# Scores of the first four head pairs as one fp32 product, with new orders of the steps: threshold attention followed by a two-layer MLP

## The chip, the cores and the metric

The kernel runs on one core of one Trainium2 chip. Its engines each work through their own queue in order and wait for one another through semaphores: TensorE (PE in the profile; its weight loads are PEld), VectorE (DVE), ScalarE (ACT), GpSimd (POOL) and SyncE (SP), of which SP and POOL here issue nearly all DMAs. The metric is the device time of one execution in microseconds (us). Three runs of the kernel before gave 519.77, 519.93 and 520.16 us, so the median is 519.93 us.

## The reference

Attention with a threshold: of each row of scores only those within tau (0.02) of the row's maximum stay, the others are masked. Then a two-layer MLP with a leaky ReLU. There are 8 batches, 8 heads, 576 positions, 64 values a head, so 64 heads, which are handled as 32 pairs; 4608 tokens of width 512, and a hidden width of 2048.

```python
scores = scale * np.matmul(q, k.transpose(0, 1, 3, 2))          # scale = 1/8
thresh = np.max(scores, axis=-1, keepdims=True) - tau
scores = np.where(scores >= thresh, scores, -1000000000.0)
scores = scores - np.max(scores, axis=-1, keepdims=True)
attn = np.exp(scores)
attn = attn / (np.sum(attn, axis=-1, keepdims=True) + 1e-09)
attn_out = np.matmul(attn, v)
x = attn_out.transpose(0, 2, 1, 3).reshape(B * S, H * D)
h = x @ w_in
out = np.maximum(0.01 * h, h) @ w_out
```

Since a score close to the threshold may fall on either side of it, the scores are needed more exactly than one fp16 product gives them.

## The kernel before, in words

Two heads make a pair (`p`, 0 to 31), and two pairs make a couple (`c`, 0 to 15). A couple has nine blocks `t` of scores: 0 to 3 are 128 query rows each of its first pair, 4 to 7 those of its second, and block 8 holds the last 64 rows of both. One pass of the main loop is a step `(c, t)`; a last pass with `c = 16` finishes what is left.

`load_qk` brings q and k of a pair into the tile `nat`, by SP's queue. `prep(p, i)` turns q (`i = 0`) or k (`i = 1`) on TensorE with an identity matrix, for the first ten pairs as plain fp32 products of 64 columns (line 151), into a pair of PSUM banks (tag `A`, of which there is one; tag `s` for the very first k). A copy on ACT scaled by 64 makes `hi` in fp16 (line 172), and a subtraction on DVE makes the rest `lo`, also in fp16 (line 175). The copy is put on the list `due`, which the letter `h` of the order runs, and the subtraction on the list `soon`, which `L` runs.

`s_mm` (line 196) makes one block of scores for both heads: for each half of the 576 columns hi times hi, lo times hi and hi times lo are added up in PSUM, for two heads side by side in the rows 0 to 63 and 64 to 127 of the array. There are two buffers `s`, one for each head, so a new block waits until DVE has read the one before. Where the step's number is in a list in line 190, the first head's six products go ahead of the second's.

`s_max` (letters `0` and `1` for the two heads) reads a block on DVE into `sn` with its extreme `nmx` (line 221), and POOL makes the threshold `nth` (line 226). Then either ACT takes the exponential `e` (line 231) and DVE masks it one step later in `s_mask` (letter `M`, line 254), or, "direct", ACT does both in `far` and `W` (lines 237 and 241). `s_mask` also issues the transposing DMA of the weights on SP (line 261). After a couple is done, its sums (`d`, `r`, `x`, `T`, `Q0`, `Q1`) and its products with v (`values`, `V0` and `V1`, line 329) follow in the next one.

MLP work comes in units: `h_unit` (four products of 512 columns, line 354, and a copy `gM` on ACT) and `out_mm` (four products, line 369; every fourth is followed by a copy on ACT and a store). The units of a batch are pushed in step 6 of every second couple from couple 2 on. `share` says how many units a step gets, `up` how they are split between the letters `U` and `u`, with `w` for one more. `filler(n)` issues n products of no use (line 126, letter `f` in the loop), with numbers for the couples 0, 1 and 2 alone.

The order of everything is written out by hand: `orders[cl][t]` is a string of these letters for each step, with `cl` = 0, 1, 2 for the first three couples, 3 for later odd ones and 4 for later even ones. Letters that work on different engines only meet through data; letters on the same engine queue up as the string has them. POOL issues the loads of v (line 107) and of the MLP weights (lines 116 and 120), ten of v's right at the start after a small copy `begun` from the first q.

Of the kernel before, what the change touches and what calls it, by code (L numbers as in the profile page):

```python
# [9 lines left out]
FP32 = mybir.dt.float32  # L10
FP16 = mybir.dt.float16
OP = mybir.AluOpType
AF = mybir.ActivationFunctionType
# [3 lines left out]
def kernel(  # L17
# [10 lines left out]
    nc = tc.nc  # L28
    B, H, S, D = q.shape
# [5 lines left out]
    NT = 9  # L35
    NJ = d_ff // 128
    QS = 64.0
# [4 lines left out]
    sb = ctx.enter_context(tc.tile_pool(name="sb", bufs=1))  # L42
# [17 lines left out]
    nat, qk, wTs, xTs = {}, {}, {}, {}  # L60
# [61 lines left out]
    def filler(n):  # L122
        if n > 0:
            t = bank()
            for _ in range(n):
                nc.tensor.matmul(out=t[:, :], lhsT=gM[:, 0, 0:128], rhs=gM[:, 0, :], start=True, stop=True,  # L126
                                 skip_group_check=True)
# [14 lines left out]
    def prep(p, i, tag="A", bufs=1):  # L142


        t = nat[p]
        pt = pair_of_banks(tag, bufs)
        for c in range(4 + i):

            if p < 10:
                for r, h in ((0, 0), (1, 0), (0, 1), (1, 1)):  # L150
                    nc.tensor.matmul(  # L151
                        out=pt[ds(64 * h, 64), r, ds((0, 2, 1, 3, 4)[c] * 64, 64)],
                        lhsT=by_head(t, i)[ds(64 * r, 64), h, c, :] if c < 4 else t[ds(64 * r, 64), 8, h, :],
                        rhs=I32[ds(64 * r, 64), ds(64 * r, 64)],
                        start=True, stop=True, skip_group_check=True,
                    )
                continue
            for r in range(2):
                nc.tensor.matmul(  # L159
                    out=pt[0:128, r, ds((0, 2, 1, 3, 4)[c] * 64, 64)],  # L160
                    lhsT=t[ds(64 * r, 64), 4 * i + c, :, :].rearrange("p h d -> p (h d)"),
                    rhs=I32[ds(64 * r, 64), ds(64 * r, 64)],
                    is_transpose=True, skip_group_check=True,
                )
# [5 lines left out]
        hi = sb.tile([128, N], FP16, tag=f"hi{i}", bufs=3, name=f"hi{i}")  # L170
        lo = sb.tile([128, N], FP16, tag=f"lo{i}", bufs=3, name=f"lo{i}")
        due.append(lambda: (nc.scalar.activation(out=by_half(hi[:, :]), in_=src, func=AF.Copy, bias=0.0, scale=QS), was.add(("hi", p, i)), soon.append(rest)))  # L172
        def rest():
            assert ("hi", p, i) in was
            nc.vector.scalar_tensor_tensor(  # L175
                out=by_half(lo[:, :]), in0=src, scalar=QS, in1=by_half(hi[:, :]),
                op0=OP.mult, op1=OP.subtract,
            )
            was.add(("lo", p, i))
        qk.setdefault(p, {})[i] = (hi, lo)  # L180

    def s_mm(c, t):


        out = [ps.tile([128, 2, 512], FP32, tag="s", bufs=2, name="s") for _ in range(2)]
        if t < 8:
            srcs = [(2 * c + t // 4, 0, ds(t % 4 * 128, 128), ds(0, 128))]
        else:
            srcs = [(2 * c + e, 1, ds(576, 64), ds(64 * e, 64)) for e in range(2)]
        hs = ((0,), (1,)) if c * NT + t in [3, 9, 10, 22, 26] else ((0, 1),)  # L190
        for hh, half in ((x, y) for x in hs for y in range(2)):
            for ti, (a, b) in enumerate(((0, 0), (1, 0), (0, 1))):
                for p, i, cols, po in srcs:
                    for h in hh:
                        r = ds(h * 64, 64)
                        nc.tensor.matmul(  # L196
                            out=out[h][po, half, 0:288], lhsT=qk[p][i][a][r, cols],
                            rhs=qk[p][1][b][r, ds(half * 288, 288)],
                            start=(ti == 0), stop=(ti == 2), skip_group_check=True,
                        )  # L200
# [233 lines left out]
    with tc.manual_schedule():  # L434
# [27 lines left out]
        share = (23, 24, 32, 13, 17, 10, 26, 35, 23, 23, 24, 26, 13, 23, 13, 26, 35, 23)  # L462
        up = [[1, 3, 2, 3, -1, -1, -1, 2, -1], [1, 3, 0, 3, -1, 1, 1, 2, -1], [2, 2, 0, 2, -3, 2, -1, 1, -1], [2, 3, 1, -1, -3, 3, -1, 1, -3], [3, 2, 0, -1, -3, 3, -1, 1, 1]]
# [3 lines left out]
        orders = [['S Pe f h 0 1 M L', 'S f h 0 1 M L', 'Pd h S f 0 1 M L', 'S 0 1 M L f', 'S f 0 L 1 M', 'S Pa f h 0 1 M L', 'S f Pb h 0 1 M L', 'S f 0 h 1 M L', 'S f 0 Pc h 1 M L'], ['S f 0 w Pd h U 1 u M L d r', 'S f 0 h x 1 u U w T L M', 'S f 0 Q0 M h U 1 u L', 'S U f 0 w V0 1 u M L', 'S f 0 U Q1 L h 1 M u', 'S f 0 1 u V1 M U L', 'S Pa f h 0 U 1 u M L', 'S f 0 U Pb w h u 1 M L', 'U S f 0 Pc h w 1 u M L'], ['S Pd f h U 0 h 1 M d L u', 'w r S f 0 U x u T h 1 M L', 'S f w L 0 Q0 h 1 U M u', 'S V0 f 0 1 M u U L w', 'S f Q1 0 U 1 h u L M', 'S f 0 V1 1 u w M U L', 'G S 0 f 1 Pa h U u M L', 'f Pb S 0 U h 1 M w u L', 'S f 0 U Pc h u M 1 L'], ['S Pd h U 0 h 1 M d w u L', 'r S 0 U x T u 1 w h L M', 'S U Q0 h 0 u 1 M L', 'S V0 0 1 u M U L', 'S 0 w L U Q1 h 1 M u', 'S V1 0 U 1 u L M', 'G S U Pa h 0 u w 1 M L', 'S 0 U Pb h u M 1 L', 'S 0 Pc h u U 1 M L w'], ['S Pd h U 0 h 1 M d w u L', 'S r 0 U x u w T h 1 M L', 'S U Q0 h 0 1 M L u', 'S V0 0 u 1 M U L w', 'S 0 w L U Q1 h 1 M u', 'S V1 0 U 1 u L M', 'G S 0 Pa U h u w 1 M L', 'S 0 U Pb h 1 u M L w', 'S 0 Pc h u U 1 M L']]  # L467
        credit = 0.0
        plan = {}

# [16 lines left out]
        for c in range(NC + 1):  # L487
            last = c == NC
            for t in range(NT):
# [21 lines left out]
                for o in orders[cl][t].split():  # L511
# [90 lines left out]
```

## Time and profile before

The profiled execution took 519.91 us, of which the profile's span is 518.1 us.

| what | number |
|---|---|
| median of three runs | 519.93 us |
| profiled execution | 519.91 us (span 518.1) |
| TensorE busy | 496.3 us, 96% |
| VectorE busy | 419.7 us, 81% |
| ScalarE busy | 428.2 us, 83% |
| GpSimd busy | 208.7 us, 40% |
| mean granted clock of TensorE | 0.988 |

In the rows of a timeline the first number is the start in us, the second the length of the group, then engine, line, instruction, and what is written from what; a bracket at the end is the idle time ahead of it on its engine and what ended it. A group row of the page ends with its count, busy time, mean in ns, and the idle time before it. The chain of waits follows the work back from the last instruction, at each step to what released it.

### The profile page before, as it was taken

What the parts mean: (1) busy time and instruction counts of PE and PEld (TensorE: products, weight loads), DVE (VectorE), ACT (ScalarE), POOL (GpSimd) and SP (SyncE); (2) the same over time, 40 slices, a digit from 0 to 9 for tenths busy, and PEclk for the clock granted to TensorE, in tenths of its full rate; (3) what the DMA queues carried; (4) which work ended last, traced back from release to release, by engine and by line L of the source; (5) the groups of instructions that cost most, each with busy time, mean ns of one, the idle gap of its engine ahead of it and who ended that gap; (6) DMA issues with size and microseconds to landing.
All of it is one profiled execution on the core that took longest, in us unless ns stands there. A gap on an engine that the chain in (4) does not pass through costs nothing.

```text
span 518.1 us, 14182 instructions
## 1 busy us (share of the span) xinstructions
PE 496.3 (96%) x5277; PEld 268.0 (52%) x5277; DVE 419.7 (81%) x1094; ACT 428.2 (83%) x777; POOL 208.7 (40%) x471
## 2 busy tenths in 40 slices
PE   7788888999999999999999999999999999999996
PEld 4354544555545565554545465555555465545444
DVE  6797998998899889987999889988999889982000
ACT  3788996988899888999898888999898888983622
POOL 6454467543553236323553336323643336320000
PEclk9798999999999999999999999999999999999999
DMA  8999999997999799988998699996998899644112
GB/s 186 162 184 185 193 174 214 176 178 133 198 179 170 134 182 174 175 149 152 180 176 159 137 185 189 158 168 134 179 174 161 136 196 149 122 92 87 40 42 61
DMA packets 260548, 80.62 MB, mean 156 GB/s; under 512 B 248704, under 2 KB 257920, under 8 KB 260480
## 3 DMA queue, kind: packets, MB, share of 16 engines
q1 hardware_dynamic: 234032, 70.68, 74.6%
q0 software_dynamic: 26368, 8.92, 18.0%
q8 instruction: 41, 0.67, 0.5%
q14 instruction: 27, 0.22, 0.1%
q10 hardware_dynamic: 80, 0.13, 0.1%
HBM read 36.70 MB, written 9.44 MB: 89 GB/s over the span
## 4 chain that ended last, share of the span: by engine, by line
PE 86%; DVE 5%; ACT 4%; issue 2%; DMA 1%; POOL 1%; SPq 0%; DVEq 0%; ACTq 0%
PE u L369 25%; PE u L354 25%; PE s L196 21%; PE A L329 8%; PE A L159 3%; DVE sn L221 3%; ACT W L241 1%; PE A L313 1%; PE A L151 1%; ACT far L237 1%; DVE W L254 1%; DMA nat<-in_q_dram 1%; PE u L126 1%; ACT hi L172 1%; ACT e L231 1%
## 5 line engine op out<-in xcount | busy, mean ns | idle before, releaser
L221 DVE TENSOR_SCALAR_CACHE_REDUCE sn<-s 128x576 f32<-128x576 f32 x288 | 208.1, 754 | 36.5 <-PE s L196 33.9
L226 POOL TENSOR_SCALAR nth<-nmx 128x1 f32<-128x1 f32 x288 | 118.0, 410 | 217.7 <-DVE sn L221 195.5
L231 ACT ACTIVATE e<-sn,nmx 128x576 f16<-128x576 f32 x190 | 143.0, 771 | 22.4 <-DVE sn L221 21.5
L254 DVE SCALAR_TENSOR_TENSOR W<-sn,nth,e 128x576 f16<-128x576 f32 x190 | 151.0, 814 | 0.4 <-POOL nth L226 0.4
L354 PE MATMUL u<-xT,win 128*128 128x512 f16 x512 | 123.9, 380 | 0.0
L369 PE MATMUL u<-wout,gM 128*128 128x512 f16 x512 | 122.3, 380 | 0.0
L196 PEld LDWEIGHTS <-hi 64*128 64x128 f16 (+1 forms) x1280 | 62.0, 97 | 63.6 <-issue 48.3
L196 PE MATMUL s<-hi,lo 64*128 64x288 f16 (+1 forms) x640 | 88.7, 285 | 0.0
L196 PE MATMUL s<-lo,hi 64*128 64x288 f16 (+1 forms) x640 | 88.5, 285 | 0.0
L237 ACT ACTIVATE far<-sn,nth 128x576 f32<-128x576 f32 x98 | 75.8, 773 | 14.0 <-POOL nth L226 12.8
L196 PE MATMUL s<-hi,hi 64*128 64x288 f16 x512 | 81.6, 290 | 5.5 <-DVE sn L221 4.9
L354 PEld LDWEIGHTS <-win 128*128 128x128 f16 x768 | 58.4, 98 | 55.0 <-issue 10.7
L358 ACT ACTIVATE gM<-u 128x512 f16<-128x512 f32 x128 | 72.5, 591 | 4.7 <-PE u L354 4.7
L369 PEld LDWEIGHTS <-gM 128*128 128x128 f16 x512 | 44.7, 98 | 53.8 <-issue 7.9
L241 ACT ACTIVATE W<-far 128x576 f16<-128x576 f32 x98 | 66.9, 683 | 3.1
L175 DVE SCALAR_TENSOR_TENSOR lo<-A,hi 128x512 f16<-128x512 f32 (+1 forms) x63 | 47.5, 755 | 10.4 <-ACT hi L172 10.3
L107 POOL DMA_DIRECT2D V<-in_v_dram x80 | 50.3, 635 | 2.7 <-DVE sn L221 1.0
L172 ACT ACTIVATE hi<-A 128x512 f16<-128x512 f32 (+1 forms) x63 | 40.1, 637 | 12.3 <-PE A L151 7.4
L329 PE MATMUL A<-wT,V 128*64 128x288 f16 x640 | 45.4, 288 | 1.1 <-ACT rc L318 1.1
L329 PEld LDWEIGHTS <-V 128*64 128x64 f16 x640 | 34.1, 109 | 11.6 <-issue 9.2
L196 PEld LDWEIGHTS <-lo 64*128 64x128 f16 (+1 forms) x640 | 31.4, 98 | 9.6 <-issue 6.1
L380 ACT ACTIVATE osb<-u 128x512 f32<-128x512 f32 x35 | 20.6, 588 | 18.8 <-PE u L369 18.4
(49 smaller groups left out, 342.6 us busy)
## 6 DMA issues: line engine op xcount, KB each, us to landing
nat<-in_q_dram SPq DMA_DIRECT2D x32, 256.0 KB, 3.7
nat<-in_k_dram SPq DMA_DIRECT2D x32, 256.0 KB, 4.2
out_dram<-osb SPq DMA_DIRECT2D x32, 256.0 KB, 3.6
V<-in_v_dram POOLq DMA_DIRECT2D x64, 64.0 KB, 4.4
wT<-W SPq DMA_TRANSPOSE x144, 4.2
win<-in_moe_w_in_dram POOLq DMA_DIRECT2D x16, 128.0 KB, 3.6
wout<-in_moe_w_out_dram POOLq DMA_DIRECT2D x16, 128.0 KB, 4.6
nat<-in_q_dram SPq DMA_DIRECT2D x32, 32.0 KB, 3.1
```

The lines of the kernel that those rows point to most:

```text
L107: nc.gpsimd.dma_start(out=Vs[b % 2][r0:r0 + 64, :, e, c0:c0 + n, :].rearrange("p g c d -> p g (c d)"), in_=rows_.rearrange("g (p c) d -> p ...
L196: nc.tensor.matmul(out=out[h][po, half, 0:288], lhsT=qk[p][i][a][r, cols], rhs=qk[p][1][b][r, ds(half * 288, 288)], start=(ti == 0), stop= ...
L221: nc.vector.tensor_scalar(out=sn[:, h, :].rearrange("p (a b) -> p a b", a=2), in0=s_[:, :, 0:288], scalar1=-BS, scalar2=None, op0=OP.mult, ...
L226: nc.gpsimd.tensor_scalar(out=nth[:, h:h + 1], in0=nmx[:, h:h + 1], scalar1=1.0, scalar2=tau_f, op0=OP.mult, op1=OP.add,)
L231: nc.scalar.activation(out=e[:, h, :], in_=sn[:, h, :], func=AF.Exp, bias=nmx[:, h:h + 1], scale=-1.0,)
L237: nc.scalar.activation(out=far[:, :], in_=sn[:, h, :], func=AF.Prelu, bias=nth[:, h:h + 1], scale=-1.0, alpha=BIG,)
L241: nc.scalar.activation(out=w[:, ds(h * 576, 576)], in_=far[:, :], func=AF.Exp, bias=0.0, scale=1.0, accum_out=dens[c][:, 2 * t + h:2 * t + ...
L254: nc.vector.scalar_tensor_tensor(out=w[:, ds(h * 576, 576)], in0=sn[:, h, :], scalar=nth[:, h:h + 1], in1=e[:, h, :], op0=OP.is_le, op1=OP ...
L329: nc.tensor.matmul(out=t[ds(h * 64, 64), half, 0:288], lhsT=vb[:, g, h, kb, :], rhs=wT[:, 4 * h + kb, ds(e * 576 + half * 288, 288)], star ...
L354: nc.tensor.matmul(out=t[:, ts(j, N)], lhsT=w_in16[:, gi, ts(j0 + j, 128)], rhs=xs[gi], start=(gi == 0), stop=(gi == NG - 1), skip_group_c ...
L358: nc.scalar.activation(out=g_out, in_=t[:, 0:nj * N].rearrange("p (j n) -> p j n", j=nj), func=AF.Prelu, bias=0.0, scale=1.0, alpha=0.01)
L369: nc.tensor.matmul(out=t[:, :], lhsT=g_in(j), rhs=w_out16[:, j, :], start=(j == 0), stop=(j == NJ - 1), skip_group_check=True,)
```

## The change

For the pairs 0 to 3 the ACT copy writes q and k scaled by 64 in fp32 into the memory that `hi` and `lo` share (one tile of `2 * N` fp16 values, seen as `N` fp32 ones); no `lo` is made, and each score product is a single fp32 product in place of three fp16 ones. These pairs are all that the couples 0 and 1 use. Pairs 4 to 31 are computed as before. Beside that, block 7 of couple 0 joins the blocks whose heads are multiplied one after the other, the numbers of fillers, `share` and `up` change in places, and the orders of ten steps change; nothing else in the loop does.

```diff
+        both = sb.tile([128, 2 * N], FP16, tag=f"x{i}", bufs=3, name=f"x{i}")[:, :]
+        if p < 4:
+            whole = both.bitcast(FP32)
+
+            def all_of_it():
+                if (p, i) in []:
+                    nc.vector.tensor_scalar(out=by_half(whole), in0=src, scalar1=QS, scalar2=None, op0=OP.mult)
+                else:
+                    nc.scalar.activation(out=by_half(whole), in_=src, func=AF.Copy, bias=0.0, scale=QS)
+                was.update((("hi", p, i), ("lo", p, i)))
+            due.append(all_of_it)
+            qk.setdefault(p, {})[i] = (whole,)
+            return
+        hi, lo = both[:, 0:N], both[:, N:2 * N]
...
-        hs = ((0,), (1,)) if c * NT + t in [3, 9, 10, 22, 26] else ((0, 1),)
+        hs = ((0,), (1,)) if c * NT + t in [3, 7, 9, 10, 22, 26] else ((0, 1),)
...
-            for ti, (a, b) in enumerate(((0, 0), (1, 0), (0, 1))):
+            terms = ((0, 0),) if srcs[0][0] < 4 else ((0, 0), (1, 0), (0, 1))
+            for ti, (a, b) in enumerate(terms):
...
-                            start=(ti == 0), stop=(ti == 2), skip_group_check=True,
+                            start=(ti == 0), stop=(ti == len(terms) - 1), skip_group_check=True,
...
-        filler(1)
+        filler(0)
         prep(0, 0)
         filler(1)
         run(take(due))
         prep(0, 1, "s", 2)
-        filler(3)
+        filler(2)
...
-        share = (23, 24, 32, 13, 17, 10, 26, 35, 23, 23, 24, 26, 13, 23, 13, 26, 35, 23)
+        share = (23, 21, 32, 13, 17, 10, 26, 35, 23, 23, 21, 26, 13, 23, 13, 26, 35, 23)
...
-        begun = sb.tile([128, 1], FP16, name="begun")
+        begun = sb.tile([128, 1], FP32, name="begun")
...
-                        filler([[0, 4, 0, 2, 6, 1, 4, 4, 3], [2, 3, 3, 2, 3, 3, 2, 4, 2], [2, 2, 4, 2, 2, 0, 0, 0, 0]][cl][t] if cl < 3 else 0)
+                        filler([[1, 5, 0, 2, 4, 1, 2, 4, 4], [2, 3, 3, 2, 3, 3, 1, 4, 4], [1, 3, 3, 1, 1, 0, 0, 0, 0]][cl][t] if cl < 3 else 0)
```

The row of `up` for couple 2 goes from `[2, 2, 0, 2, -3, 2, -1, 1, -1]` to `[1, 2, 0, 2, -3, 2, -3, 1, -1]`. The steps whose order changes, as `cl,t`:

```diff
-0,0 S Pe f h 0 1 M L
+0,0 S Pe f h M 0 1 L
-1,3 S U f 0 w V0 1 u M L
+1,3 S U f 0 V0 1 u M L
-2,3 S V0 f 0 1 M u U L w
+2,3 S f V0 0 1 M u U L w
-2,6 G S 0 f 1 Pa h U u M L
+2,6 G S 0 f 1 Pa h U u L M
-2,7 f Pb S 0 U h 1 M w u L
+2,7 f Pb S 0 U h 1 M w L u
-3,3 S V0 0 1 u M U L
+3,3 S 0 V0 1 u M U L
-3,7 S 0 U Pb h u M 1 L
+3,7 S 0 U Pb h M 1 u L
-4,1 S r 0 U x u w T h 1 M L
+4,1 r S 0 U x u w T h 1 M L
-4,3 S V0 0 u 1 M U L w
+4,3 S 0 V0 u 1 M U L w
-4,7 S 0 U Pb h 1 u M L w
+4,7 S 0 U Pb h 1 M L u w
```

More of the change, by code (lines that the diff above doesn't have):

```diff
@@ L466 @@
         d1n = [[1, 4, 6, 7], [0, 1, 4, 5, 6, 7, 8], [0, 1, 2, 3, 5, 7], [0, 3, 5, 6, 7], [3, 5, 6, 7, 8]]
-        orders = [['S Pe f h 0 1 M L', 'S f h 0 1 M L', 'Pd h S f 0 1 M L', 'S 0 1 M L f', 'S f 0 L 1 M', 'S Pa f h 0 1 M L', 'S f Pb h 0 1 M L', 'S f 0 h 1 M L', 'S f 0 Pc h 1 M L'], ['S f 0 w Pd h U 1 u M L d r', 'S f 0 h x 1 u U w T L M', 'S f 0 Q0 M h U 1 u L', 'S U f 0 w V0 1 u M L', 'S f 0 U Q1 L h 1 M u', 'S f 0 1 u V1 M U L', 'S Pa f h 0 U 1 u M L', 'S f 0 U Pb w h u 1 M L', 'U S f 0 Pc h w 1 u M L'], ['S Pd f h U 0 h 1 M d L u', 'w r S f 0 U x u T h 1 M L', 'S f w L 0 Q0 h 1 U M u', 'S V0 f 0 1 M u U L w', 'S f Q1 0 U 1 h u L M', 'S f 0 V1 1 u w M U L', 'G S 0 f 1 Pa h U u M L', 'f Pb S 0 U h 1 M w u L', 'S f 0 U Pc h u M 1 L'], ['S Pd h U 0 h 1 M d w u L', 'r S 0 U x T u 1 w h L M', 'S U Q0 h 0 u 1 M L', 'S V0 0 1 u M U L', 'S 0 w L U Q1 h 1 M u', 'S V1 0 U 1 u L M', 'G S U Pa h 0 u w 1 M L', 'S 0 U Pb h u M 1 L', 'S 0 Pc h u U 1 M L w'], ['S Pd h U 0 h 1 M d w u L', 'S r 0 U x u w T h 1 M L', 'S U Q0 h 0 1 M L u', 'S V0 0 u 1 M U L w', 'S 0 w L U Q1 h 1 M u', 'S V1 0 U 1 u L M', 'G S 0 Pa U h u w 1 M L', 'S 0 U Pb h 1 u M L w', 'S 0 Pc h u U 1 M L']]
+        orders = [['S Pe f h M 0 1 L', 'S f h 0 1 M L', 'Pd h S f 0 1 M L', 'S 0 1 M L f', 'S f 0 L 1 M', 'S Pa f h 0 1 M L', 'S f Pb h 0 1 M L', 'S f 0 h 1 M L', 'S f 0 Pc h 1 M L'], ['S f 0 w Pd h U 1 u M L d r', 'S f 0 h x 1 u U w T L M', 'S f 0 Q0 M h U 1 u L', 'S U f 0 V0 1 u M L', 'S f 0 U Q1 L h 1 M u', 'S f 0 1 u V1 M U L', 'S Pa f h 0 U 1 u M L', 'S f 0 U Pb w h u 1 M L', 'U S f 0 Pc h w 1 u M L'], ['S Pd f h U 0 h 1 M d L u', 'w r S f 0 U x u T h 1 M L', 'S f w L 0 Q0 h 1 U M u', 'S f V0 0 1 M u U L w', 'S f Q1 0 U 1 h u L M', 'S f 0 V1 1 u w M U L', 'G S 0 f 1 Pa h U u L M', 'f Pb S 0 U h 1 M w L u', 'S f 0 U Pc h u M 1 L'], ['S Pd h U 0 h 1 M d w u L', 'r S 0 U x T u 1 w h L M', 'S U Q0 h 0 u 1 M L', 'S 0 V0 1 u M U L', 'S 0 w L U Q1 h 1 M u', 'S V1 0 U 1 u L M', 'G S U Pa h 0 u w 1 M L', 'S 0 U Pb h M 1 u L', 'S 0 Pc h u U 1 M L w'], ['S Pd h U 0 h 1 M d w u L', 'r S 0 U x u w T h 1 M L', 'S U Q0 h 0 1 M L u', 'S 0 V0 u 1 M U L w', 'S 0 w L U Q1 h 1 M u', 'S V1 0 U 1 u L M', 'G S 0 Pa U h u w 1 M L', 'S 0 U Pb h 1 M L u w', 'S 0 Pc h u U 1 M L']]
         credit = 0.0
```

4 lines of the change are left out of this document (1 added, 3 removed).

## The prediction

> **What bounds the kernel now.** I read the page first, then busy time by windows, then the chain of waits for the first 90 us, then the timelines of ScalarE (ACT) and VectorE (DVE) there. "Step (c,t)" is score block t of pair couple c; "hole" is idle time ahead of an instruction.
>
> ```profile
> span 518.1 us, 14182 instructions
> PE 496.3 (96%) x5277; PEld 268.0 (52%) x5277; DVE 419.7 (81%) x1094; ACT 428.2 (83%) x777; POOL 208.7 (40%) x471
> PE   7788888999999999999999999999999999999996
> ...
> 17.75:24.57 6.82, 5.32 (x26) 2.12 (x28) 5.49 (x15) 5.39 (x10) 2.93 (x6) 0.50 1.18 184
> 41.64:45.05 3.41, 3.32 (x16) 1.33 (x16) 2.66 (x8) 3.02 (x7) 1.65 (x5) 0.50 0.71 134
> 45.05:90.00 44.95, 38.14 (x600) 22.96 (x598) 40.03 (x105) 37.66 (x70) 27.22 (x59) 1.00 1.28 194
> 90.00:510.00 420.00, 420.00 (x4189) 225.24 (x4182) 345.19 (x901) 359.47 (x653) 158.37 (x360) 1.00 0.90 151
> ```
>
> The window rows give length, then busy time of PE, weight loads, DVE, ACT, POOL, then the granted clock. From 90 to 510 us TensorE (PE) has no hole: 420.00 of 420.00. Its queue there is a fixed list that the change does not shorten, since pairs 4 to 31 keep their three products. So the end moves by as much as the moment moves at which PE becomes full, and that moment is set earlier, where no engine is full and where PE is given 65 idle products (the fillers of line 126) to keep its clock up; twice the clock was granted at 0.50 all the same. The question is what sets the pace before 90 us, and there ACT and DVE share it:
>
> ```profile
> 5.66 6.29 POOL L107 DMA_DIRECT2D V<-in_v_dram  x10
> 13.73 0.78 ACT L237 ACTIVATE far<-sn,nth 128x576 f32<-128x576 f32 x1 [1.91 <-POOL nth L226]
> 19.22 0.78 ACT L237 ACTIVATE far<-sn,nth 128x576 f32<-128x576 f32 x1 [0.52 <-POOL nth L226]
> 22.22 0.78 ACT L237 ACTIVATE far<-sn,nth 128x576 f32<-128x576 f32 x1 [0.75 <-POOL nth L226]
> 25.78 0.60 ACT L172 ACTIVATE hi<-A 128x512 f16<-128x512 f32 x1 [1.32 <-PE A L151]
> 41.97 0.78 ACT L237 ACTIVATE far<-sn,nth 128x576 f32<-128x576 f32 x1 [1.60 <-POOL nth L226]
> ...
> L237 ACT ACTIVATE far<-sn,nth 128x576 f32<-128x576 f32 x10 | 7.7, 771 | 5.6 <-POOL nth L226 5.6
> L172 ACT ACTIVATE hi<-A 128x640 f16<-128x640 f32 (+1 forms) x5 | 3.2, 649 | 1.6 <-PE A L151 1.6
> ```
>
> The last two rows group ACT's work between 13.6 and 42 us. Its holes there are 5.6 + 1.6 = 7.2 us, and 1.9 of them is the first row's; 5.3 us stand between 13.73 and 41.97. In all other time of this stretch ACT runs without a break. ACT's own work does not fall in the change, so these 5.3 us are the most that can be won there. What stands behind them:
>
> ```profile
> 16.42 0.28 PE L196 MATMUL s<-lo,hi 64*128 64x288 f16 x1
> ...
> 17.41 0.82 DVE L175 SCALAR_TENSOR_TENSOR lo<-A,hi 128x640 f16<-128x640 f32 x1 [1.66 <-ACT hi L172]
> 25.13 0.76 DVE L221 TENSOR_SCALAR_CACHE_REDUCE sn<-s 128x576 f32<-128x576 f32 x1 [1.88 <-PE s L196]
> 39.74 0.82 DVE L175 SCALAR_TENSOR_TENSOR lo<-A,hi 128x640 f16<-128x640 f32 x1 [1.18 <-ACT hi L172]
> ...
> 7.45 0.84 DVE lo L175
> 8.32 0.80 PE s L196 x10
> 9.15 1.46 DVE sn L221 x4
> ...
> 19.64 1.59 PE s L196 x11
> 21.24 2.67 PE u L126 x6
> 23.91 1.23 PE s L196 x12
> 26.62 0.89 PE s L196 x11
> 27.52 0.97 PE u L126 x4
> ...
> 63.59 1.43 DVE sn L221 x4
> ```
>
> Twice DVE stands in its queue at a `lo` (line 175) until ACT has got to the `hi` before it, while the scores behind it in DVE's queue have long been ready (those of step (0,3) with the row at 16.42). And the hole at 25.13 is a chain on PE at half clock: six fillers in 2.67 us ahead of the scores that DVE waits for (four take 0.97 at full clock).
>
> **The change part by part.**
>
> *The `lo` instructions.* Eight go (two for each of pairs 0 to 3).
>
> ```profile
> L175 DVE SCALAR_TENSOR_TENSOR lo<-A,hi 128x640 f16<-128x640 f32 x31 | 25.5, 823 | 8.5 <-ACT hi L172 8.5
> L175 DVE SCALAR_TENSOR_TENSOR lo<-A,hi 128x512 f16<-128x512 f32 x32 | 22.0, 688 | 1.9 <-ACT hi L172 1.8
> L172 ACT ACTIVATE hi<-A 128x512 f16<-128x512 f32 x32 | 18.7, 583 | 9.6 <-PE A L151 6.9 <-PE A L159 2.6
> L380 ACT ACTIVATE osb<-u 128x512 f32<-128x512 f32 x35 | 20.6, 588 | 18.8 <-PE u L369 18.4
> ```
>
> That is 4 x 823 + 4 x 688 ns = 6.0 us of DVE work. ACT's copy stays and writes fp32 in place of fp16; by the last two rows (588 against 583 ns for the same count) that costs nothing. The little copy `begun` on POOL also reads fp32 now, one column, nothing. The bank of the transposes comes free after ACT's copy instead of after `lo`, so later transposes in PE's queue start sooner.
>
> *The products.* Per score block 12 fp16 products go and 4 fp32 ones come (24 and 8 in block 8). The trace has no fp32 product of 288 columns; nearest are the transposes by a product with the identity, 64 columns, fp32:
>
> ```profile
> 8.58 0.39 PE L196 MATMUL s<-hi,hi 64*128 64x288 f16 x2
> ...
> 8.71 0.39 PE L196 MATMUL s<-hi,lo 64*128 64x288 f16 x2
> ...
> 9.14 0.69 PE L151 MATMUL A<-I,nat 64*64 64x64 f32 x32
> ...
> 12.44 0.81 PE L151 MATMUL A<-I,nat 64*64 64x64 f32 x40
> ```
>
> The fp32 product shows as two instructions: 16 calls, 32 records. Eight records more, which are four calls running side by side in four parts of the array, take 0.81 - 0.69 = 0.12 us for 64 columns. Scaled to 288 columns that is 0.54 us for both heads of one half block, against 3 x 0.13 = 0.39 for the three fp16 pairs (8.58 to 8.71). So +0.15 a half, +0.3 us for each of the 18 blocks of c = 0 and 1: 5.4 us of PE time. Lower bound: if the 0.12 is the issue of 16 records (loads included) and not columns, 2 x 0.13 = 0.26 a half, a gain of 0.26 a block. Upper bound: the two heads run one after the other, 1.08 a half, +1.4 a block. I take +0.3, because the nearest rows run side by side in the same row parts and scale with columns at half clock too (four fillers against six above). [...]
>
> This PE time lies in the stretch where PE has holes and fillers, so it counts only as latency, where DVE waits for scores. Fillers fall from 65 to 60, 5 x 0.24 = 1.2 us by the 0.97 row.
>
> *The start.* The chain 7.45 to 9.13 loses the `lo` (0.84) and its block gets 0.3 longer: first scores 0.5 us earlier; in step (0,1) the other `lo` was hidden behind the scores, so +0.3, and 0.2 is left. Nothing of it counts: ACT's 13.73 waits for POOL, which issues ten loads of v until 11.95 from the first copy of q on, and that copy is where it was. From 13.73 I start to count.
>
> *Steps (0,3) and (1,1).* DVE's 1.66 + 0.82 before the scores of (0,3) go; late next are these scores themselves, 16.7 + 0.3 = 17.0 us, so DVE gets on about 1.1 us earlier than 17.41 + 0.82, and ACT's 0.52 closes. Likewise 1.18 + 0.82 = 2.0 before (1,1) go, more than ACT's 1.60 there.
>
> *Steps (0,4), (0,5).* Six fillers become four, and PE's idle time before 19.64, behind which the clock had halved, shrinks with the earlier scores, while every block keeps PE busy 0.3 longer. I take the clock as kept: fillers 0.97, scores 0.89 + 0.3 in place of 2.67 and 1.23: 1.7 us less on the chain that made DVE's 1.88. ACT's 0.75 and 1.32 close. If the clock halves again, the fillers still lose 0.9 but the block is 2.4, and little of the two holes closes. [...]
>
> *The four small holes* (5.3 - 0.5 - 0.75 - 1.3 - 1.6 = 1.15 us together) stand behind waits for scores, which get 0.3 longer, and behind transposes, which come earlier: I count half, 0.6. Sum of the stretch: 0.5 + 0.75 + 1.3 + 1.6 + 0.6 = 4.75.
>
> *The rest of c = 1*: scores are 0.3 longer, pairs 4 and 5 keep their `lo`. ACT has only short holes there; I take two of them as deeper: +0.6. If ACT covers all, 0; if each of the seven blocks shows, +2.1.
>
> *Couple 2.* In (2,3) a filler pair behind `values` becomes one ahead of it, where PE waits for ACT anyway:
>
> ```profile
> 71.75 1.42 PE A L329 x20
> 73.17 0.54 PE u L126 x2
> 73.70 0.85 PE s L196 x9
> ...
> 81.18 1.90 PE L354 MATMUL u<-xT,win 128*128 128x512 f16 x8
> ```
>
> The 0.54 leave the chain; DVE's hole after it is 0.42, so 0.4 is won. The other fillers of c = 2 stand ahead of waits for DVE, so 0.
>
> *New orders later, share, up.* Steps (odd,7) put the second head's softmax ahead of the MLP units' copies in ACT's queue, which makes copies at most one softmax later; the units there are output products, of which one in four needs a copy: 0. Its cover is PE's full queue; without it a copy comes up to 1.5 us late (`far` and `W`), +1.5 for each of seven such steps. The other moves (M in (0,0), `values` or the reciprocal against scores and "0", L or M against units) pass no instruction of their own engine, apart from stores and transposes that change places in SP's queue, hidden by the same cover. `lo` before the masks in (2,6) still waits for ACT's `hi`: 0. Block (0,7) by heads: its first head needs only the first buffer free, a gain under 0.3 that I leave in the small holes. `share` and `up` spread the same units otherwise over the steps: 0, by the same cover.
>
> Sum: -4.75 + 0.6 - 0.4 = -4.55. The profiled execution took 519.91 us (span 518.1, 1.8 around it), the median of three is 519.93: 515.3 us, span 513.5.
>
> **The rivals.**
> *Half:* the clock halves again, or ACT's large holes at (0,4), (0,5) find another cause (POOL's issue of loads between two `nth`). Then only 0.5 + 1.6 + 0.4 - 0.6 remain: 518.0. For it: the idle 1.9 us of POOL's making at 13.73 show that POOL can hold ACT.
> *Larger:* fp32 products are at the lower bound and close all holes of the stretch and of c = 1 as well, another 1.5 to 2: 513.5.
> *Slower, products one after the other:* fp32 products of the two heads do not overlap. A block is 2.2 us; DVE's step is then two `sn` (1.46) + 2.2 = 3.7 us where c = 0 and 1 now take 54.4/18 = 3.0 (sn at 9.15 to 63.59): +0.65 x 18 = +12, less 2 of the above: 530. It decides from a block of about 1.6 us. Against it: the four-way overlap in L151's rows.
> *Does nothing or slower, given back later:* PE full for 420 us has no slack, so a new order that makes PE wait 0.7 us in each of seven rounds of two couples eats all: 520 to 522. Against it: those moves cross queues, not within PE.
>
> **How the numbers follow.** Main 0.60 (513.9 to 517.0), half 0.17 (517.0 to 519.0), larger 0.07, given back 0.10, one after the other 0.06. The range for 8 in 10 is 513.4 to 519.0; it leaves out the two slower cases and a little below. A measurement tells 0.2% (1.0 us) from no change: faster than 518.9 is main, larger and nearly all of half, 0.83; within, 0.05; slower, 0.12.
>
> **What would show it.** Line 175 with 55 instructions; 160 fp32 records on line 196 (80 calls), about 0.5 us a half block; no `lo` wait at (0,3) and (1,1); ACT without a hole over 0.5 us between 13.7 and the first far of (1,1), which comes near 37.2 instead of 41.97; clock 1.00 throughout; first MLP product (row 81.18) near 76.6; still 100% PE from 90 on. Wrong: a block over 1.6 us, clock at 0.50, or PE holes after 90.

## The result and the profile after

The changed kernel takes 517.11 us (median of four runs, 516.95 to 517.55) where the kernel before takes 519.85 us in runs on the same chip (519.66 to 520.16). The ratio is 0.9948, 95% interval 0.9931 to 0.9965: it is faster by 0.5%. The forecast was 515.3 us, so the direction came out and the time lies 1.8 us above it, inside the range of 513.4 to 519.0. It is just outside the band of 513.9 to 517.0 that the forecast gave to its own mechanism, in the band of "half", a clock that halves again; that did not happen, as the next rows show.

The profiled execution took 516.95 us. Line numbers of the changed kernel are 6 to 13 higher: `s_mm` is line 209, `lo` line 187, the fp32 copy line 178, `sn` line 234, `far` line 250, `values` line 342, the transposing DMA line 274, the stores line 417. The page of the profile after, its first parts:

```profile
span 515.1 us, 14003 instructions
PE 498.1 (97%) x5192; PEld 270.2 (52%) x5192; DVE 414.4 (80%) x1086; ACT 428.0 (83%) x777; POOL 208.2 (40%) x471
PE   7999888998999999999999999999999999999996
PEclk9999999999999999999999999999999999999999
```

PE works 1.8 us more than before, DVE 5.3 us less, and the clock, once it is on (8.32 us), does not fall again until 513.49. The stretch that was to be won, by windows, and then ACT's group row and timeline in it (after):

```profile
13.70:37.00 23.30, 22.31 (x256) 12.62 (x249) 19.51 (x55) 22.35 (x41) 13.07 (x29) 1.00 1.18 191
85.00:510.00 425.00, 423.62 (x4227) 227.16 (x4228) 345.73 (x902) 360.59 (x656) 158.78 (x361) 1.00 0.90 150
```

```profile
L250 ACT ACTIVATE far<-sn,nth 128x576 f32<-128x576 f32 x10 | 7.7, 769 | 2.4 <-POOL nth L239 2.3
...
13.71 0.78 ACT L250 ACTIVATE far<-sn,nth 128x576 f32<-128x576 f32 x1 [1.98 <-POOL nth L239]
18.58 0.77 ACT L250 ACTIVATE far<-sn,nth 128x576 f32<-128x576 f32 x1
21.10 0.78 ACT L250 ACTIVATE far<-sn,nth 128x576 f32<-128x576 f32 x1 [0.28 <-POOL nth L239]
23.36 0.60 ACT L178 ACTIVATE x<-A 128x512 f32<-128x512 f32 x1
37.03 0.78 ACT L250 ACTIVATE far<-sn,nth 128x576 f32<-128x576 f32 x1
```

ACT does 22.35 us of work between 13.70 and the `far` of step (1,1), 22.57 before by this window of the kernel before:

```profile
13.70:41.97 28.27, 21.75 (x287) 11.23 (x282) 22.87 (x60) 22.57 (x42) 13.08 (x30) 0.87 1.07 177
```

So the same work fits into 23.3 us in place of 28.3: the holes at (0,3), (0,4), (0,5) and (1,1) are gone or nearly so, and the `far` of (1,1) starts at 37.03 where it was 41.97.

How much earlier each step runs can be read from the start of the first head's `sn` on DVE. After minus before, in us:

| step | (0,0) | (0,2) | (0,4) | (0,5) | (1,1) | (2,0) | (2,3) | (2,4) | (3,0) | (4,3) | (4,4) | (15,8) |
|---|---|---|---|---|---|---|---|---|---|---|---|---|
| difference | 0.00 | +0.70 | -1.11 | -2.88 | -4.93 | -3.90 | -3.90 | -4.40 | -4.44 | -4.45 | -3.01 | -3.03 |

By the end of couple 2 the gain is 4.44 us. It stands unchanged up to (4,3), and in one step 1.4 us of it go, for good. The window row from 85 us on shows the same: 423.62 of 425.00, a hole of 1.38 us where PE had been full. The chain of waits there (after), PE's timeline (after), and PE's timeline of the kernel before at the same place:

```profile
121.21 6.63 DMA wT<-W
```

```profile
127.89 0.80 PE L342 MATMUL A<-wT,V 128*64 128x288 f16 x10 [1.38 <-DMA wT<-W]
```

```profile
130.16 1.55 PE L329 MATMUL A<-wT,V 128*64 128x288 f16 x20
...
136.37 1.42 PE L329 MATMUL A<-wT,V 128*64 128x288 f16 x20
```

The first half of `values` of couple 3 (letter `V0` in step (4,3)) needs, for its last ten products, the transposed weights of block (3,8). After the change they land 6.63 us after their DMA's issue and PE waits 1.38 us. Before, the products took 1.55 us at that place where the second half (the last row) takes 1.42, and the transfer landed at 130.86, while they ran: there too it arrived only just in time. It had no slack to lose.

Why did it land late? SP's timeline, first after, then before:

```profile
119.93 1.19 SPq L417 DMA_DIRECT2D out_dram<-osb  x2
121.21 2.71 SPq L274 DMA_TRANSPOSE wT<-W  x1
```

```profile
124.39 1.19 SPq L404 DMA_DIRECT2D out_dram<-osb  x2
125.67 2.72 SPq L261 DMA_TRANSPOSE wT<-W  x1
```

Everything up to the issue is 4.46 us earlier. But the DMA needs 6.63 us in place of 5.19 (issue at 125.67, landed at 130.86). Two suspects stand in the profile: the store of the first 256 rows, which is queued on SP just ahead of the transposing DMA in both kernels, and a load of instructions, which falls into the flight only after the change. The DMA view from 124.2 to 127.9 us after (what was moved in 40 equal slices, then queues with packets, MB and share), and its queue row beside q1 from 125.67 to 130.9 before, which is the whole flight:

```profile
GB/s 125 152 133 91 58 39 28 42 39 282 241 263 235 25 19 8 0 0 0 6 8 6 11 8 11 8 8 11 19 263 293 272 267 296 288 293 285 230 255 230
...
q1 hardware_dynamic: 1708, 0.43, 118.7%
q8 instruction: 1, 0.02, 1.6%
```

```profile
q14 instruction: 1, 0.01, 0.4%
```

Queue q8 brings instructions 16 KB at a time, 41 times in the execution (0.67 MB). I take them to be PE's: over its 10,384 products and weight loads that is some 65 bytes each, and the run with the fewest of these (10,224) has 40 such loads, the one with the most (10,600) has 42. After the change one such load starts 3.87 us after the transposing DMA's issue; before, the nearest ones are 2.6 us ahead of the issue and 6.9 us behind it. In the slices (0.0925 us each) the load begins in the tenth, and from the fourteenth to the twenty-ninth, 1.5 us, almost nothing is moved, with the transposing DMA still under way. The change takes some 170 instructions from PE's list, so the load comes at another place of the work.

### The profile page after: what moved, and what is told of

It is laid out like the page before. It is cut to its first block, busy times and chain, and to the rows that moved or that the text cites. A ratio compares the mean times of both kernels' runs of the same rounds, so it can differ in the third digit from the quotient of the medians.

```text
span 515.1 us, 14003 instructions
## 1 busy us (share of the span) xinstructions
PE 498.1 (97%) x5192; PEld 270.2 (52%) x5192; DVE 414.4 (80%) x1086; ACT 428.0 (83%) x777; POOL 208.2 (40%) x471
## 4 chain that ended last, share of the span: by engine, by line
PE 89%; DMA 3%; ACT 3%; DVE 3%; issue 1%; POOL 1%; DVEq 0%; ACTq 0%; POOLq 0%
PE u L367 25%; PE u L382 25%; PE s L209 23%; PE A L342 8%; PE A L159 3%; DMA wT<-W 3%; PE u L126 2%; PE A L151 2%; DVE sn L234 1%; PE A L326 1%; ACT far L250 1%; ACT W L254 1%; ACT e L244 1%; DVE W L267 1%; DMA nat<-in_q_dram 1%
## 5 line engine op out<-in xcount | busy, mean ns | idle before, releaser
L239 POOL TENSOR_SCALAR nth<-nmx 128x1 f32<-128x1 f32 x288 | 117.5, 408 | 215.8 <-DVE sn L234 194.3
L209 PE MATMUL s<-x,x 64*128 64x288 f16 (+1 forms) x1472 | 128.4, 298 | 1.9 <-DVE sn L234 1.9
L209 PEld LDWEIGHTS <-x 64*128 64x128 f16 (+1 forms) x1680 | 66.2, 96 | 59.5 <-issue 46.4
L187 DVE SCALAR_TENSOR_TENSOR x<-A,x 128x512 f16<-128x512 f32 (+1 forms) x56 | 42.2, 754 | 7.2 <-ACT x L184 7.1
L184 ACT ACTIVATE x<-A 128x512 f16<-128x512 f32 (+1 forms) x56 | 35.7, 638 | 5.6 <-PE A L159 4.7
L355 DVE TENSOR_TENSOR xT<-A,rc 128x576 f16<-128x576 f32 x32 | 24.1, 755 | 8.9 <-PE A L342 8.9
L359 POOL COPY xE<-xT 128x64 f16<-128x64 f16 x32 | 14.3, 448 | 30.1 <-DVE xT L355 30.1
```

What stands on the lines that cost most here:

```text
L209: nc.tensor.matmul(out=out[h][po, half, 0:288], lhsT=qk[p][i][a][r, cols], rhs=qk[p][1][b][r, ds(half * 288, 288)], start=(ti == 0), stop= ...
L239: nc.gpsimd.tensor_scalar(out=nth[:, h:h + 1], in0=nmx[:, h:h + 1], scalar1=1.0, scalar2=tau_f, op0=OP.mult, op1=OP.add,)
```

## The experiments

The step table's difference against the kernel before is used throughout, "slack" is the time between the landing of the transposed weights and the eleventh product of `V0`. The first four runs tell apart the parts of the change, and the fourth takes the wait away.

**Products alone.** Old fillers, `share`, `up`, list of line 202 and orders, fp32 products kept:

```diff
-        orders = [['S Pe f h M 0 1 L', ...
+        orders = [['S Pe f h 0 1 M L', ...
-        filler([[1, 5, 0, 2, 4, 1, 2, 4, 4], ...
+        filler([[0, 4, 0, 2, 6, 1, 4, 4, 3], ...
```

> The change's products alone: q and k of pairs 0 to 3 in fp32 and one fp32 product per score, with the fillers, orders, share, up and the list of split blocks as before. Theory A (the eight subtractions on VectorE stood in its queue ahead of finished scores): the stands at steps (0,3) and (1,1) are gone, ScalarE's holes there close, couple 2 starts at least 3 us earlier than before (first sn of couple 2 at 60.5 us or less, 63.59 before), 516.5 to 518.0 us. Theory B (the new fillers and orders give the gain, by the clock): the blocks cost 0.3 us more each and little is won, 519.5 us or more, with the clock at 0.50 in two stretches as before.

Measured: 517.72 us, ratio 0.9959 (0.9946 to 0.9972). The steps run 4.68 us earlier at (1,1), 3.64 in couple 3 and 2.24 from (4,4) on; the clock stays at 1.00. So the fp32 products carry most of the gain without any new order, and the wait at (4,3) comes with them too (the DMA lands 6.60 us after its issue). It is not made by the new orders.

**Orders alone.** `hi` and `lo` and three products for all pairs, everything else as after:

```diff
-        if p < 4:
+        if p < 0:
...
-            terms = ((0, 0),) if srcs[0][0] < 4 else ((0, 0), (1, 0), (0, 1))
+            terms = ((0, 0),) if srcs[0][0] < 0 else ((0, 0), (1, 0), (0, 1))
```

> The change without its products: all pairs keep hi and lo and three fp16 products, with the new fillers, orders, share, up and split block. Theory A: the subtractions still hold VectorE at (0,3) and (1,1); only the filler moved ahead of values in (2,3) gives 0.4 us, and four fillers in place of six up to 1 us: 518.5 to 520.5 us. Theory B: 517.0 to 518.0 us, with the clock at 1.00.

Measured: 519.00 us, ratio 0.9985 (0.9967 to 1.0003): no gain that can be told from none. The clock falls to 0.50 twice (17.95 to 24.78 and 41.85 to 48.67), and ACT's holes ahead of `far` are as large as before:

```profile
L250 ACT ACTIVATE far<-sn,nth 128x576 f32<-128x576 f32 x10 | 7.7, 771 | 5.8 <-POOL nth L239 5.8
```

The steps are 1.03 late at (2,0) and 0.53 late at (2,4): the filler moved ahead of `values` in (2,3) is worth 0.5 here as in the change. This profiled execution took 520.28 us, where the ten runs went from 517.89 to 520.72, so its steps need not hold for all of them.

**Subtractions kept.** fp32 products, but the old subtraction is still issued, into a tile that nobody reads:

```diff
                 was.update((("hi", p, i), ("lo", p, i)))
+                soon.append(dead)
+
+            def dead():
+                d = sb.tile([128, N], FP16, tag=f"d{i}", bufs=1, name=f"d{i}")
+                nc.vector.scalar_tensor_tensor(
+                    out=by_half(d[:, :]), in0=src, scalar=QS, in1=by_half(whole),
+                    op0=OP.mult, op1=OP.subtract,
+                )
```

> The changed kernel, but VectorE still makes an unused lo for pairs 0 to 3 (eight instructions of the old size, at their old places, into a tile that nobody reads), so the fp32 products and all orders stay and VectorE's work and its stands come back. Theory A: ScalarE's holes at (0,3) and (1,1) come back and the blocks are still 0.3 us longer, 519.5 to 521.5 us. Theory B: VectorE's work does not matter, 516.9 to 517.6 us.

Measured: 521.66 us, ratio 1.0034 (1.0016 to 1.0051). DVE's timeline and ACT's group row of this kernel:

```profile
17.55 0.82 DVE L184 SCALAR_TENSOR_TENSOR d<-A,x 128x640 f16<-128x640 f32 x1 [1.21 <-ACT x L178]
37.94 0.82 DVE L184 SCALAR_TENSOR_TENSOR d<-A,x 128x640 f16<-128x640 f32 x1 [1.18 <-ACT x L178]
...
L258 ACT ACTIVATE far<-sn,nth 128x576 f32<-128x576 f32 x10 | 7.7, 771 | 5.4 <-POOL nth L247 5.4
```

With the subtraction in its queue DVE stands for ACT's copy again, ACT's holes are back at 5.4 us, and most of the gain is gone at (1,1) already, -1.37 in place of -4.93; at (2,0) it is +0.07, but there a fall of the clock to 0.50 from 40.90 to 44.32 counts as well. What makes the kernel faster is that the subtraction is gone, not the fp32 product. The subtraction also held the bank of the transposes, and this run brings that back too; in the kernel before it makes TensorE wait 0.3 us once between 9 and 45 us (its weight loads 0.8), so the stand of DVE is the larger part. That the longer products cost time by themselves does not follow from the +0.34%: up to (4,3) this run is 0.49 us ahead of the kernel before, and it loses 1.47 us in that step. The transposed weights land late here as well (6.66 us after the issue, with an instruction load 3.95 us behind it), though they are issued at 125.17, close to the 125.67 of the kernel before: it is not the hour that counts but what else is in flight.

**Store behind.** As after, but the two stores of the first 256 rows are issued after the transposing DMA of block (3,8):

```diff
+                if b == 0 and u == 0:
+                    held.append(go)
+                else:
+                    go()
...
+                            if prev == (3, 8):
+                                run(take(held))
```

> The changed kernel with one store (rows 0 to 255 of the output) issued behind the transposing DMA of block (3,8) instead of ahead of it in SyncE's queue; nothing else moves. Theory C (the 1.4 us that values waits in step (4,3) come from this transpose being issued late, behind a store that waits for ScalarE): the transpose is issued about 2 us earlier, TensorE does not wait there, 515.6 to 516.0 us, and the start of the first sn of couple 5 is 4.4 us ahead of the kernel before instead of 3.0. Theory D (the transfers themselves are slow in that stretch whatever their order): the wait stays, 516.8 to 517.5 us.

Measured: 515.32 us, ratio 0.9916 (0.9889 to 0.9943). SP's and PE's timelines:

```profile
116.31 4.50 SPq L274 DMA_TRANSPOSE wT<-W  x2
120.91 1.19 SPq L419 DMA_DIRECT2D out_dram<-osb  x2
...
126.24 1.42 PE L342 MATMUL A<-wT,V 128*64 128x288 f16 x20
```

The DMA is issued at 119.52, lands at 122.70 with 4.2 us of slack, and `V0` runs through in 1.42 us. Without the wait of (4,3) the time is 1.8 us lower and at the forecast value; 1.4 of these are the wait. It does not show yet whether the store or the instruction load made the late landing, for both have gone: the load now starts 4.47 us after the issue, when the weights have landed.

**Which pairs.** Only pairs 1 and 3 in fp32, then only pairs 0 and 2, then pairs 0 to 5; all three with the store behind:

```diff
+    WHOLE = (1, 3)       # (0, 2); (0, 1, 2, 3, 4, 5)
...
-        if p < 4:
+        if p in WHOLE:
```

> The changed kernel with the store behind the transpose, and only pairs 1 and 3 in fp32; pairs 0 and 2 keep hi, lo and three products. Theory A (what counts is the two stands of VectorE at (0,3) and (1,1), whose subtractions belong to pairs 1 and 3): ScalarE's holes there close as in the changed kernel, most of the 4.4 us stays, 515.5 to 517.5 us. Theory E (the gain goes by VectorE's work, half of the subtractions, half of the gain): 517.5 to 518.2 us.

> The same with pairs 0 and 2 in fp32 in place of 1 and 3. Theory A: the stands at (0,3) and (1,1) remain with 0.5 and 1.6 us of ScalarE holes, the gain at couple 2 is 1.5 us or less, 518.3 to 520 us. Theory E: 517.5 to 518.2 us.

> The changed kernel with the store behind the transpose, and pairs 4 and 5 in fp32 too, so couple 2 as well. Theory A (VectorE sets the pace of couple 2 up to step (2,6), and the subtractions of pairs 4 and 5 lie in that chain): another 1 to 2 us, 513.3 to 514.6 us. Theory F (ScalarE and the longer score blocks set it): within 0.6 us of the kernel with four pairs, 514.8 to 516.0 us.

Measured: 515.44 us with pairs 1 and 3 (ratio 0.9924, 0.9901 to 0.9946), 519.15 with pairs 0 and 2 (0.9978, 0.9963 to 0.9993), 515.92 with six pairs (0.9924, 0.9909 to 0.9939). ACT's group row with pairs 1 and 3, then with pairs 0 and 2:

```profile
L255 ACT ACTIVATE far<-sn,nth 128x576 f32<-128x576 f32 x12 | 9.2, 768 | 2.2 <-POOL nth L244 2.1
```

```profile
L255 ACT ACTIVATE far<-sn,nth 128x576 f32<-128x576 f32 x11 | 8.5, 769 | 6.1 <-POOL nth L244 6.1
20.49:23.90 3.41, 3.41 (x19) 1.60 (x16) 2.79 (x8) 2.71 (x7) 1.99 (x4) 0.50 1.03 172
```

The two stands of DVE, ahead of the scores of (0,3) and (1,1), are subtractions of pairs 1 and 3. Doing these two pairs alone closes ACT's holes and takes the steps to -5.20 in couple 3, more than the change's -4.44, with the blocks of the other two pairs as short as before. Doing the other two keeps the holes, and the clock falls to 0.50 (the second row and another stretch from 40.97 to 47.79).

With six pairs the steps are at -4.66 at (2,0), 0.76 better than after (0.30 of it is an earlier first block), and at -4.38 at (3,0): couple 2 gives it back. PE's busy time from (2,0) to (3,0), with four pairs (store behind) and with six:

```profile
60.23:88.90 28.67, 23.86 (x354) 14.34 (x357) 25.93 (x70) 23.37 (x44) 19.19 (x41) 1.00 1.31 202
```

```profile
58.93:88.41 29.48, 26.51 (x318) 15.30 (x321) 25.43 (x68) 23.46 (x44) 19.13 (x41) 1.00 1.23 196
```

PE has 2.65 us more work in this couple and is busy 90% of it (83% with four pairs), and the couple takes 0.81 us longer. That the longer products are no longer hidden there is the likely reading, not a tested one. The further gain of theory A did not come.

**No fillers in couple 0.** Its 23 fillers go, with the store behind:

```diff
-                        filler([[1, 5, 0, 2, 4, 1, 2, 4, 4], [2, 3, 3, ...
+                        filler([[0, 0, 0, 0, 0, 0, 0, 0, 0], [2, 3, 3, ...
```

> The changed kernel with the store behind the transpose, and no fillers in couple 0 (23 before). Theory G (the fp32 products keep the clock up by themselves, and fillers ahead of scores are on the chain of couple 0): clock 1.00, up to 1.5 us faster, 513.8 to 515.3 us. Theory H (without fillers the clock is halved again): stretches at 0.50 before 45 us, 516.5 us or more.

Measured: 515.89 us, ratio 0.9921 (0.99 to 0.9942), against 0.9916 with them. The clock is at 0.50 from 17.28 to 27.52, and the steps are at -3.06 at (3,0) by its profile, an execution of 516.67 us where the four runs went from 514.32 to 516.67. The medians differ by only 0.6 us, less than the intervals can tell. With the clock at 0.50 for 10 us most of the gain is still there, so an unbroken clock is not what makes it. What the fillers of couple 0 are worth beside the fp32 products stays open.

**Fillers cut.** As after, with the store where it was, but the 34 fillers of couples 1 and 2 in three instructions each, the same columns in all. This adds 68 products and 68 weight loads to PE's list ahead of (4,3), and no work:

```diff
-                nc.tensor.matmul(out=t[:, :], lhsT=gM[:, 0, 0:128], rhs=gM[:, 0, :], ...
+                for x0, x1 in zip(cuts, cuts[1:]):
+                    nc.tensor.matmul(out=t[:, x0:x1], lhsT=gM[:, 0, 0:128], rhs=gM[:, 0, x0:x1], ...
...
+        (0, 172, 344, 512) if c in (1, 2) else (0, 512)
```

> The changed kernel with its store where it was, and each of the 34 fillers of couples 1 and 2 cut into three products of 172, 172 and 168 columns: the same columns for TensorE, but 136 more instructions in its queue (68 products and 68 weight loads) before couple 3. Theory I (the transpose of block (3,8) lands 1.4 us later in the changed kernel because one of the 16 KB instruction loads falls into its flight, 3.9 us after its issue; that moment is set by how many instructions TensorE has used up): the load comes about 5 us earlier, 1 to 2 us ahead of the issue, the transpose lands after 5.2 us as in the kernel before, TensorE waits at most 0.2 us there, 515.4 to 516.2 us. Theory J (fp32 in memory or something else of the products makes that transpose slow): it lands after 6.6 us, TensorE waits 1.4 us, 516.9 to 517.6 us.

Measured: 516.28 us, ratio 0.992 (0.9897 to 0.9943). The queue row of the DMA view from 117.5 to 122.1 us, then SP's and PE's timelines:

```profile
q8 instruction: 1, 0.02, 1.2%
```

```profile
122.11 2.71 SPq L275 DMA_TRANSPOSE wT<-W  x1
126.60 1.53 PE L343 MATMUL A<-wT,V 128*64 128x288 f16 x20
```

The instruction load now starts at 119.5, 2.6 us ahead of the issue, as in the kernel before. With the store still ahead of it the DMA lands in 5.18 us, as before, and `V0` takes 1.53 us, 0.1 more than with slack. So the 1.4 us come from the instruction load that falls into the flight. The store ahead has a price of its own: without a load in flight the DMA of block (3,8) takes 5.15 to 5.19 us behind it (three profiles) and 3.18 to 3.21 ahead of it (six). This execution's clock came on only at 10.16 us (8.32 after), which put the first block 0.83 late; 0.89 of that are left at (4,3), which fits a time a little above what was expected.

**Pairs 1 and 3, with fillers cut.** The run with pairs 1 and 3 had waited 0.98 us much later, at step (13,3). Its chain of waits, PE's timeline and the DMA view's queue row (383.2 to 385.9 us) there:

```profile
381.09 5.10 DMA wT<-W
```

```profile
386.23 0.80 PE L347 MATMUL A<-wT,V 128*64 128x288 f16 x10 [0.98 <-DMA wT<-W]
```

```profile
q8 instruction: 1, 0.02, 2.2%
```

It is the same pair of a transposing DMA (block (12,8)) and an instruction load within its flight. The cut fillers move that load as well:

> Pairs 1 and 3 alone in fp32, the store behind the transpose, and the same 34 fillers cut in three. Theory I: the instruction load that fell into the flight of the transpose of block (12,8), where values waited 1.0 us, moves by some 5 us, that wait goes, 514.0 to 514.8 us. Theory J: the wait at couple 13 stays, 515.0 to 515.8 us.

Measured: 514.86 us (514.71 to 515.82), ratio 0.9902 (0.9881 to 0.9922). PE's timeline at (13,3):

```profile
384.55 1.42 PE L348 MATMUL A<-wT,V 128*64 128x288 f16 x20
```

The instruction load now starts 3.22 us ahead of the DMA's issue, the DMA lands after 3.37 us, and the wait is gone. By its median this kernel is the fastest of the study, 1.0% below the kernel before, where the changed kernel is 0.5% below it; its interval overlaps those of several others.

**One fp16 product.** As after with the store behind, but pairs 0 to 3 keep only `hi`, in fp16, and one product. The terms with `lo` are left out, so the scores of these pairs are less exact:

```diff
-                    nc.scalar.activation(out=by_half(whole), in_=src, ...)
+                    nc.scalar.activation(out=by_half(both[:, 0:N]), in_=src, ...)
-            qk.setdefault(p, {})[i] = (whole,)
+            qk.setdefault(p, {})[i] = (both[:, 0:N],)
```

> The changed kernel with the store behind the transpose, where pairs 0 to 3 use hi times hi alone, one fp16 product per score; the terms with lo are left out for them, so their scores are rougher. It shows what the length of the fp32 products still costs: a block is 0.25 us of TensorE instead of about 1.0. Theory K (blocks are latency that VectorE waits for, at least at (0,1), (1,5) and (1,6)): 0.5 to 1.5 us faster than with fp32, 513.8 to 514.8 us. Theory L (less work for TensorE lets its clock fall and nothing is won): 515 us or more, with a stretch at 0.50 before 45 us.

Measured: 515.87 us, ratio 0.9922 (0.9899 to 0.9945), against 0.9916 with fp32 products. The granted clock by windows:

```profile
14.35:28.00 13.65, 10.87 (x102) 4.04 (x102) 10.55 (x31) 12.36 (x24) 7.56 (x19) 0.50 1.08 182
```

Taking most of the product time away wins nothing: the clock falls to 0.50 for 17 us (the row and 41.66 to 45.07). Some of the missing gain has another cause: this run, too, meets an instruction load in the flight of block (12,8) (3.05 us after the issue; it lands after 5.11) and loses 0.5 us at (13,3). Without that it would be about level with the fp32 products. So in the changed kernel their length costs nothing that a shorter product would win back with these orders; that the length of the fp32 products is what keeps the clock up is the likely reading, but only this one run speaks for it.

## Why the prediction was right in direction, and where it was wrong

**The stretch to couple 2** came out by its steps. Forecast -4.75 up to the first `far` of (1,1), measured -4.94 (41.97 to 37.03; 37.2 was forecast). Then +0.6 for the rest of couple 1, measured +1.03 between (1,1) and (2,0), so the term was 0.4 too small. Then -0.4 for the filler in (2,3), measured -0.50. In sum -4.55 against -4.44, closer than its terms: they are off by 0.2, 0.4 and 0.1, partly against one another, which is luck. Two of the signs named came as well: the first MLP product at 76.76 us (76.6 was forecast), and no hole of ACT over 0.28 us behind the first. The mechanism, DVE standing at `lo` with ready scores behind it, is borne out by the run that keeps the subtraction, and the run with pairs 1 and 3 alone shows that the two places named were the ones.

**The products.** The changed kernel's group rows, fillers and a block of the chain at 1.00 of the clock, and a block of PE's timeline:

```profile
L209 PE MATMUL s<-x,x 64*128 64x288 f32 x128 | 25.0, 439 | 0.9 <-DVE sn L234 0.9
L209 PE MATMUL s<-x 64*64 64x288 f32 x32 | 2.8, 410 | 0.0
L187 DVE SCALAR_TENSOR_TENSOR x<-A,x 128x640 f16<-128x640 f32 x28 | 23.0, 822 | 5.7 <-ACT x L184 5.7
L187 DVE SCALAR_TENSOR_TENSOR x<-A,x 128x512 f16<-128x512 f32 x28 | 19.2, 686 | 1.5 <-ACT x L184 1.4
...
19.84 0.97 PE u L126 x4
40.72 1.17 PE s L209 x8
...
51.86 1.89 PE L209 MATMUL s<-x,x 64*128 64x288 f32 x8
```

There are 160 fp32 records, as forecast. A block takes 1.17 us where it took 0.89: +0.28, forecast +0.3, and 0.585 a half block where 0.54 was worked out from the transposes. But 1.17 us holds only where both heads can run side by side. At 51.86 the second head's products start 0.65 us after the first's, when DVE has read their buffer (up to 52.4), and the block takes 1.89; four others of the two couples take 1.8 us or more, and a block over 1.6 was named as a sign of being wrong. The forecast had no term for this, and it may be what made +0.6 into +1.03. `lo` counts 28 + 28 = 56, not 55: 63 instructions stood before by the two rows quoted, with one more in the group that writes from the very first k, so 64 less 8. The four fillers at (0,4) took 0.97 us, so the clock was kept as forecast; in the run without couple 0's fillers it fell at 17.28. In the kernel before it had fallen at 17.75, for 6.82 us, and at 41.64, for 3.41; in the 3.4 us ahead of these falls PE was busy for 2.1 us (14.33 to 17.75) and 1.4 us (38.22 to 41.64).

**The start.** First scores were to come 0.5 us earlier and to count for nothing. In this execution, whose clock came on at 8.32 us instead of 7.50, they came 0.00 earlier; in the run without couple 0's fillers, with the clock on at 7.04, 0.49. Step (0,1) was to lose 0.3 and lost 0.72; with the old four fillers (products alone) it lost 0.50, so the fifth filler made 0.22 of it. Behind 13.71 ACT has no hole up to 18.58 and took that up. But a shift of the first scores does count, against the forecast. Four profiles share the orders and products of couple 0: six pairs, after, store behind and fillers cut. Their clock came on at 7.80, 8.32, 9.61 and 10.16 us, their first scores at -0.30, 0.00, +0.54 and +0.83, and their first `far` at 13.41, 13.71, 14.25 and 14.54. That after's 13.71 is so near the 13.73 of before is chance.

**The orders.** "0" was right: they made PE wait nowhere, so the rival "given back later" had the wrong cause. The run with the old orders loses the same time at the same place. Of the other rivals, products one after the other fell with the block of 1.17 us (it decided from 1.6) and, since some blocks are longer, with the step of couples 0 and 1, 2.8 us (first scores from 9.15 to 59.69, 18 steps) where that rival had 3.7, "half" with the clock at 1.00 and the closed holes, and "larger" with the +1.03 in couple 1.

**The step that failed** is the first: from 90 to 510 us PE has no hole, "so the end moves by as much as the moment moves at which PE becomes full". A full engine has no hole, but that says nothing of the slack of the transfers it is about to need. In the kernel before the transposed weights of block (3,8) came with none (`V0` took 1.55 in place of 1.42 us, a row of the trace that the prediction leaves out), and of the signs of being wrong that were named, "PE holes after 90" is one that came: 1.38 us at 126.5. The term that was missing is +1.4. With the transposing DMA issued ahead of the store there is slack, and the time is the forecast one, 515.32 against 515.3; by the ratios to the kernel before it is 0.9916 against 0.9911.

**What stays open.** Why an instruction load of 16 KB delays a transposing DMA by over a microsecond is shown in part. By its row in the window above, 1.6% of 16 engines over 3.7 us, the load keeps a DMA engine busy for about 0.95 us, from 125.08 on. For 0.8 us after that (126.0 to 126.8, the DMA view of after) packets start only one by one:

```profile
q1 hardware_dynamic: 28, 0.01, 8.5%
```

In the 0.8 us that follow 831 start. It looks as if the transposing DMA had to wait until the engine with the load had caught up; the profile does not say on which engine a packet runs, so this is a reading and not shown.

## What to carry to other kernels

When an engine is full, look for the transfers that reach it with no slack before you move the whole programme earlier: a product group that takes 0.13 us longer than its twin was such a place here, and reordering one queue so that the urgent transfer goes first is cheap (517.11 to 515.32 us). An instruction that stands in an in-order queue ahead of ready work can keep its engine from that work for longer than its own length (1.66 us of standing ahead of the 0.82 of the `lo` at 17.41), and here the four of two pairs were worth as much as all eight (515.44 against 515.32 us). Fewer instructions on one engine also moved the instruction loads against everything else here (some 170 fewer put one 3.87 us behind the issue of a transposing DMA, and PE waited 1.38 us), so a difference of a microsecond between two close versions may be that alone.

## What the runs showed of the hardware

- Transposing DMAs with a load of instructions in their flight land later. After 60 us in the changed kernel, the 31 transposing DMAs with a q8 load starting 1 to 4.2 us behind their issue land in 4.85 us in the median, the other 96 in 3.85; in the kernel before 4.97 (30 of them) and 4.03 (98). There are 41 such loads in an execution of either kernel, 0.67 MB in all; the 1.4 us at (4,3) are what one of them cost TensorE there.
- The same work with 136 instructions more in PE's list was no slower, by its median faster: 0.992 of the time before (0.9897 to 0.9943) against 0.9948 (0.9931 to 0.9965).
- The clock came on between 6.77 and 10.16 us after the start in the profiles shown here. In the four that share couple 0 the first scores moved with it by up to 1.1 us, and so did the first `far`; the 0.83 us of the latest against after were still there at (4,3) (0.89).
- The stretches at 0.50 before 60 us in these profiles lasted 3.41 us (41.64 to 45.05 in the kernel before) or two, three or four times that (17.75 to 24.57 there, 17.28 to 27.52 without couple 0's fillers, 14.35 to 28.00 with one fp16 product). Counted in windows of 3.41 us from the moment the clock came on, all ten falls came after a window in which PE was busy 28 to 62% of the time. The least busy windows without a fall had 53, 58 and 59%.
